# Other transfer and load times in a schedule table, and new seeds, in a two-layer MoE kernel behind attention

## The chip, the core and the metric

The kernel runs on one core of one Trainium2 chip. The metric is the device time of one execution in microseconds (us). Of the kernel before there are three timed executions and one more that was profiled.

The engines are named as the profile names them: PE is TensorE (PEld its weight loads), ACT is ScalarE, DVE is VectorE, POOL is GpSimd, SP is SyncE. Each engine works through its own list of instructions in the order in which the program put them there, and waits at an instruction whose inputs are not ready.

## The reference

Causal attention on 2 x 12 heads of 448 positions and 64 columns, then two feed-forward layers on the 896 tokens, each 768 to 2048 to 768:

```python
scores = scale * np.matmul(q, k.transpose(0, 1, 3, 2))
scores = np.where(mask, -1000000000.0, scores)
...
attn = attn / (np.sum(attn, axis=-1, keepdims=True) + 1e-09)
x = np.matmul(attn, v)                       # heads side by side: 896 x 768

h = x @ w_in                                 # layer 0
x = (h * np.clip(h + 3.0, 0.0, 6.0) / 6.0) @ w_out
h = x @ w_in2                                # layer 1
y = (np.maximum(h, 0.0) + alpha * np.minimum(h, 0.0)) @ w_out2
```

The four weight matrices are float64, everything else is float32.

## The kernel before

**Attention.** `attend` handles a head pair of both batches, six times: scores (line 496), the row maximum on DVE (447), exponentials on ACT (452), normalising on POOL or DVE (467 to 476), transposes on PE (521), copies of these from PSUM to SBUF on ACT or DVE (547 and 554), and the product with v (565).

**The two layers** use a seven-product scheme for 2 x 2 blocks instead of eight. Every product multiplies a sum of weight blocks by a sum of activation blocks, and every float32 operand is split in a high and a low part, so that `three` (584) issues three matmuls of 448 columns for each 128 x 128 block. Layer 0 and layer 1 have the same shape: first `w_in`, eight pairs of row blocks, 63 matmuls each, then `w_out`, seven products of 72 matmuls in the order 1, 2, 7, 6, 4, 5, 3.

**Preparing weights.** `convert` loads a block of float64 words (SP, 259) into one of three `raw` buffers and makes float32 of it in two ACT instructions (262 and 265) and one on DVE (268). In `w_in` the sums of blocks are `s12` (599 and 601) and two sums in place, made by `add_on`: `w1 += s12` and `w2 += w1`. Then come casts to the high part on ACT (617) and the subtraction that gives the low part on DVE (618). The products' tiles are named after these: `a1`, `s12`, `s4`, `s3`, `a2`; the pair's results stand in the PSUM banks `a`, `b` and `c` and are copied out by ACT (319 and 321, to a tile `g`) before the bank takes the next product; the results are then added up (650) and passed through the activation function (660 to 668). In `w_out` the right-hand sides of products 7, 6 and 4 are sums in place of `g` tiles (again `add_on`), split into `x70h`, `x60h`, `x40h` and so on (283 on ACT, 290 on DVE), and its weights are `w7h`, `w6h` and so on.

**A sum in place** (`add_on`, 301) has two forms: a DMA that adds to its destination, issued by POOL (307), or an addition on DVE (309).

**The order** is worked out by a planner in the kernel (`Plan.solve`, 113). It keeps a time for each engine and takes, step by step, the instruction that can start first, the earlier due time first. Each operation carries a cost in us. A transfer is counted as landing `WAIT[cols]` plus 0.0025 us a column after its issue, a load after the two numbers in its `.lands(...)`, and due times are counted back through these. For a sum in place the planner chooses the engine:

```python
if POOL in o.dma and done_by(*o.on[0]) + o.on[-1][1] <= o.due - EARLY:
    ok = e == POOL
else:
    ok = e == min(o.on, key=lambda c: done_by(*c))[0]
```

So it is a transfer if that would be done 3 us (`EARLY`) and one addition before it is due, and otherwise goes to whichever of the two is done first. The due times of the attention's operations are shaken by a random number generator started from each of `SEEDS` in turn.

Of the kernel before, what the change touches and what calls it, by code (L numbers as in the profile page):

```python
# [24 lines left out]
W3 = HK * P  # L25
# [7 lines left out]
PE, DVE, ACT, POOL, SP = "PE", "DVE", "ACT", "POOL", "SP"  # L33


def f32(t):
    return t.bitcast(F32)
# [23 lines left out]

ISSUE, WAIT = 0.9, {384: 2.2, 448: 4.6, 768: 4.2}

TURN = {("r", "r"): 0.05, ("r", "t"): 0.17, ("r", "c"): 0.2, ("r", "q"): 0.15, ("r", "m"): 0.15, ("t", "r"): 0.12,
        ("t", "c"): 0.12, ("t", "q"): 0.1, ("m", "c"): 0.2, ("m", "r"): 0.1, ("m", "q"): 0.1}
# [14 lines left out]
class Plan:  # L82
# [4 lines left out]
    def op(self, on, emit, reads=(), writes=(), due=FAR, chain=None, also=(), port=False, mode=None):  # L87

        o = Op(on if isinstance(on, list) else [on], emit, due)
        o.port, o.mode = port, mode  # L90
        for key in reads:
            w, r = self.state.setdefault(key, ([], []))
            o.before.update(w)
            r.append(o)
        for key in writes:
            w, r = self.state.setdefault(key, ([], []))
            o.before.update(w)
            o.before.update(r)
            self.state[key] = ([o], [])
        o.before.discard(o)  # L100
        for key in (*reads, *writes, *also):
            b = key[0] if isinstance(key, tuple) else key
            if b not in o.bufs:
                o.bufs.append(b)
                b.left += 1
        if chain:
            if chain in self.last:
                o.before.add(self.last[chain])
            self.last[chain] = o
        self.ops.append(o)  # L110
        return o
# [127 lines left out]
class Kernel:  # L239
# [9 lines left out]
    def convert(self, src, sign=1.0, halves=False):  # L249

        nc, op = self.nc, self.plan.op
        raw = Buf("raw", "raw", 2 * DM, U32)
        w = Buf("w", "wf", DM, U32)
        keys = [(w, 0), (w, W3)] if halves else [w]

        def words(k):
            return raw.tile.rearrange("p (n two) -> p n two", two=2)[:, :, k]

        op((SP, 0.45), lambda e: nc.sync.dma_start(out=raw.tile, in_=src), writes=[(raw, "l"), (raw, "h")]).lands(2.3, 1.9)


        op((ACT, 0.80), lambda e: nc.scalar.activation(  # L262
            f32(w.tile), f32(words(1)), AF.Prelu, scale=sign * 2.0 ** -112, alpha=-2.0 ** 32), reads=[(raw, "h")], writes=keys)

        op((ACT, LOWEST), lambda e: nc.scalar.activation(  # L265
            words(0), raw.tile.bitcast(U16).rearrange("p (n four) -> p n four", four=4)[:, :, 1],
            AF.Copy, bias=-0.49999, scale=1.0 / 8192.0), writes=[(raw, "l")])
        op((DVE, 0.87), lambda e: nc.vector.scalar_tensor_tensor(  # L268
            out=w.tile, in0=w.tile, scalar=3, in1=words(0), op0=ALU.logical_shift_left, op1=ALU.bitwise_or),
           reads=[(raw, "l")], writes=keys, port=True)  # L270
        return w
# [26 lines left out]
        op(low_on, low, reads=[*keys, hi], writes=[lo], port=not ps)  # L298
        return hi, lo

    def add_on(self, out, cols, dst, src, reads, writes, send=False):

        nc = self.nc

        def emit(e):
            if e == POOL:
                nc.gpsimd.dma_start(out=dst(), in_=src(), accum_op=ALU.add)  # L307
            else:
                nc.vector.tensor_add(dst(), dst(), src())

        on = [(POOL, ISSUE), (DVE, 0.065 + 0.00105 * cols)]
        self.plan.op(on[:1] if send else on, emit, reads=reads, writes=writes, port=True).lands(WAIT[cols], 0.0025 * cols, on=POOL)

    def copy(self, out, src, key, cols, sign=1.0):
        nc = self.nc
# [276 lines left out]
    def w_in(self, layer, m, src, due):  # L592
        nc, op = self.nc, self.plan.op
        w1 = self.convert(src[m], -1.0, True)
        w2 = self.convert(src[m + PAIRS], 1.0, True)
        s12 = Buf("w", "s12", DM, F32)
        left, right = slice(0, W3), slice(W3, DM)

        op((DVE, 0.47), lambda _: nc.vector.tensor_add(s12.tile[:, right], f32(w2.tile[:, left]), f32(w2.tile[:, right])),  # L599
           reads=[(w2, 0), (w2, W3)], writes=[(s12, W3)], port=True)  # L600
        op((DVE, 0.47), lambda _: nc.vector.tensor_add(s12.tile[:, left], s12.tile[:, right], f32(w1.tile[:, left])),  # L601
           reads=[(s12, W3), (w1, 0)], writes=[(s12, 0)], port=True)

        def both(name, cols, src, keys):

            if cols == DM:
                hi, lo = Buf("w", name + "h", DM, F32R), Buf("w", name + "l", DM, F32R)
                parts = (hi, 0), (lo, 0)
            else:
                t = Buf("w", name, DM, F32R)  # L610
                parts = ((t, 0), 0), ((t, W3), W3)

            def out(i):
                key, first = parts[i]
                return (key[0] if isinstance(key, tuple) else key).tile[:, first:first + cols]

            op((ACT, 0.07 + 0.00087 * cols), lambda _: nc.scalar.copy(out(0), src()), reads=keys, writes=[parts[0][0]])  # L617
            op((DVE, 0.065 + 0.00105 * cols), lambda _: nc.vector.tensor_sub(out(1), src(), f32(out(0))),  # L618
               reads=[*keys, parts[0][0]], writes=[parts[1][0]], port=True)
            return parts  # L620
# [2 lines left out]
        p56 = both("s12", DM, lambda: s12.tile, [(s12, 0), (s12, W3)])  # L623
        p4 = both("a2", W3, lambda: f32(w2.tile[:, right]), [(w2, W3)])

        self.add_on(w1, W3, lambda: f32(w1.tile[:, right]), lambda: s12.tile[:, left], [(s12, 0)], [(w1, W3)], SEND > 1)
        self.add_on(w2, W3, lambda: f32(w2.tile[:, left]), lambda: f32(w1.tile[:, left]), [(w1, 0)], [(w2, 0)], SEND > 0)
        p7 = both("s4", W3, lambda: f32(w1.tile[:, right]), [(w1, W3)])
        p3 = both("s3", W3, lambda: f32(w2.tile[:, left]), [(w2, 0)])

# [193 lines left out]
WARM = 3  # L824
SPLIT = (0, 1)
SEND = 0
LOWEST = 0.85
SCALERS = 2
SEEDS = (21, 46993, 49846, 39502, 10980, 46964, 66667)
ATT = {"kq": 2 * S, "v": 8 * D, "e": 3 * P, "el": 4 * P, "small": 21, "a": 16 * P}  # L830


def solve(k):
    return k.plan.solve(SLOTS, ("u", "w", "raw"), ("u", OVER, set(ATT)), k.vary, SEEDS)

# [105 lines left out]
```

## Time and profile before

| | |
|---|---|
| three timed executions | 526.29, 525.88, 526.03 us (median 526.03) |
| the profiled execution | 521.06 us, its span from first to last instruction 519.0 us |
| busy share of the span | PE 96%, PEld 83%, DVE 82%, ACT 75%, POOL 25% |
| matmuls | 2598, of which 2016 in the two layers (line 584) |
| moved by DMA | 82.69 MB |

The span is one core's. Matmuls overlap in the pipeline, so the busy share of PE doesn't tell how near it is to its peak; idle time that the profile shows on PE is lost, though. The clock of PE (PEclk in the views) is 1.00 at the full 2.4 GHz and 0.50 at 1.2 GHz. Attention fills the first 84 us, `w_in` of layer 0 runs on PE from there to 193 us, `w_out` from 193 to 304, layer 1's `w_in` to 411 and its `w_out` to 516 us.

### The profile page before, as it was taken

Reading aid. Unit: us, or ns where it says so; the run is one execution under the profiler, and the core shown is the slowest. Engines: PE = TensorE matmul, PEld = TensorE weight load, DVE = VectorE, ACT = ScalarE, POOL = GpSimd, SP = SyncE. Lnnn points to the kernel's source line nnn. Section 1 sums busy time; section 2 is a strip of 40 time slices with the busy share of each in tenths; the row PEclk is TensorE's granted clock in tenths of the full one; section 3 lists DMA queues with packets and bytes.
Section 4 is the critical chain, followed back from the end, with each engine's and each line's share of the span. In section 5 each row is a group of like instructions: output and inputs, shape, how many; then the busy total and the mean of one; then the engine's idle time right before and its main releaser. Section 6 shows DMA issues by size and latency. Waiting matters only on the chain.

```text
span 519.0 us, 7641 instructions
## 1 busy us (share of the span) xinstructions
PE 496.6 (96%) x2598; PEld 429.2 (83%) x2598; DVE 425.1 (82%) x808; ACT 390.5 (75%) x756; POOL 128.7 (25%) x196
## 2 busy tenths in 40 slices
PE   8899999999799999998998897999999999989997
PEld 4575667989689999997997786889999999979996
DVE  5799989999588799878999986887787999699710
ACT  6999999888588799866966676777788997597101
POOL 2775884112111003621001011221210146200000
PEclk9999999999889999999999899999999999999999
DMA  8655300678766549998005436676764699930111
GB/s 273 261 197 167 90 21 24 189 216 218 188 168 167 192 136 276 256 267 251 11 0 153 136 85 162 188 204 148 198 160 153 200 258 273 249 75 1 54 53 53
DMA packets 27638, 82.69 MB, mean 159 GB/s; under 512 B 3152, under 2 KB 15184, under 8 KB 27600
## 3 DMA queue, kind: packets, MB, share of 16 engines
q1 hardware_dynamic: 15216, 61.76, 34.3%
q0 software_dynamic: 12384, 20.45, 22.4%
q8 instruction: 20, 0.33, 0.3%
q14 instruction: 18, 0.15, 0.1%
HBM read 59.00 MB, written 2.75 MB: 119 GB/s over the span
## 4 chain that ended last, share of the span: by engine, by line
PE 44%; DVE 27%; DMA 17%; issue 5%; ACT 5%; POOL 2%; DVEq 0%; POOLq 0%; ACTq 0%; SPq 0%
PE a L584 12%; PE ya L584 12%; DMA g<-g 8%; PE c L584 7%; DMA wf<-s 6%; DVE wf L268 4%; PE b L584 3%; PE yc L584 3%; PE o L565 2%; PE t L521 2%; PE s L496 2%; DVE e L447 2%; DVE g L662 2%; DMA raw<-w2o 1%; DMA raw<-w1o 1%
## 5 line engine op out<-in xcount | busy, mean ns | idle before, releaser
L307 POOL DMA_DIRECT2D g<-g x48 | 41.6, 925 | 146.2 <-DVE g L668 50.3
L268 DVE SCALAR_TENSOR_TENSOR wf<-wf,raw 128x768 uint32<-128x768 uint32 x64 | 60.9, 952 | 15.1 <-ACT wf L262 14.9
L265 ACT ACTIVATE raw<-raw 128x768 uint32<-128x768 uint16 x64 | 58.5, 916 | 4.5 <-DMA raw<-w2i 1.9
L262 ACT ACTIVATE wf<-raw 128x768 f32<-128x768 f32 x64 | 57.5, 903 | 2.8 <-DVE w3l L287 1.4
L307 POOL DMA_DIRECT2D wf<-wf x25 | 21.8, 871 | 133.5 <-DVE s L599 39.4
L452 ACT ACTIVATE e<-e,small 128x128 f32<-128x128 f32 (+2 forms) x72 | 36.0, 505 | 5.1 <-DVE small L447 4.9
L476 POOL TENSOR_SCALAR e<-e,small 128x256 f32<-128x256 f32 (+2 forms) x67 | 31.4, 492 | 15.6 <-DVE small L469 11.0
L447 DVE CUSTOM_DVE_ANT_0 e<-s,mask 128x384 f32<-128x384 f32 (+2 forms) x72 | 27.0, 419 | 6.1 <-PE s L496 5.5
L618 DVE TENSOR_TENSOR s<-wf,s 128x384 fp32r<-128x384 f32 x32 | 17.8, 570 | 10.2 <-ACT s L617 10.2
L319 ACT COPY o<-ya 128x448 f32<-128x448 f32 x3 | 1.6, 533 | 31.6 <-PE ya L584 31.6
L617 ACT CAST s<-wf 128x384 fp32r<-128x384 f32 x32 | 16.1, 507 | 12.0 <-DMA wf<-s 10.2
L565 PE MATMUL o<-a,v 128*64 128x448 f32 (+3 forms) x192 | 23.4, 386 | 0.0
L617 ACT CAST s12h<-s 128x768 fp32r<-128x768 f32 x16 | 13.3, 834 | 13.1 <-DVE s L601 13.1
L565 PEld LDWEIGHTS o<-a,v 128*64 128x64 f32 x192 | 12.7, 136 | 12.6 <-issue 5.2
L496 PE MATMUL s<-kq 64*128 64x384 f32 (+2 forms) x144 | 21.7, 405 | 1.3 <-DMA kq<-kq 0.8
L618 DVE TENSOR_TENSOR s12l<-s,s12h 128x768 fp32r<-128x768 f32 x16 | 15.8, 988 | 7.2 <-ACT s12h L617 6.7
L521 PE MATMUL t<-ident,e 128*128 128x128 f32 x144 | 19.0, 278 | 1.6 <-DVE small L447 1.1
L521 PEld LDWEIGHTS t<-ident,e 128*128 128x128 f32 x144 | 15.5, 141 | 5.5 <-POOL e L476 2.4
L496 PEld LDWEIGHTS s<-kq 64*128 64x128 f32 x144 | 11.6, 186 | 9.2 <-DVE small L447 3.2
L307 POOL DMA_DIRECT2D wf<-s x13 | 11.2, 864 | 25.3 <-DVE s L618 10.7
L668 DVE SCALAR_TENSOR_TENSOR g<-r,alpha,g 128x448 f32<-128x448 f32 x24 | 16.3, 679 | 0.9 <-ACT r L666 0.8
L319 ACT COPY g<-a 128x448 f32<-128x448 f32 x16 | 8.5, 531 | 10.3 <-PE a L584 10.1
(830 smaller groups left out, 1771.3 us busy)
## 6 DMA issues: line engine op xcount, KB each, us to landing
raw<-w1i SPq DMA_DIRECT2D x16, 768.0 KB, 5.4
raw<-w1o SPq DMA_DIRECT2D x16, 768.0 KB, 4.4
raw<-w2i SPq DMA_DIRECT2D x16, 768.0 KB, 4.5
raw<-w2o SPq DMA_DIRECT2D x16, 768.0 KB, 5.0
g<-g POOLq DMA_DIRECT2D x48, 224.0 KB, 9.1
kq<-kq SPq DMA_DIRECT2D x11, 448.0 KB, 5.3
wf<-wf POOLq DMA_DIRECT2D x10, 384.0 KB, 8.8
v<-v SPq DMA_DIRECT2D x12, 256.0 KB, 2.7
```

The source lines that it names most:

```text
L262: op((ACT, 0.80), lambda e: nc.scalar.activation(f32(w.tile), f32(words(1)), AF.Prelu, scale=sign * 2.0 ** -112, alpha=-2.0 ** 32), reads= ...
L265: op((ACT, LOWEST), lambda e: nc.scalar.activation(words(0), raw.tile.bitcast(U16).rearrange("p (n four) -> p n four", four=4)[:, :, 1], A ...
L268: op((DVE, 0.87), lambda e: nc.vector.scalar_tensor_tensor(out=w.tile, in0=w.tile, scalar=3, in1=words(0), op0=ALU.logical_shift_left, op1 ...
L307: nc.gpsimd.dma_start(out=dst(), in_=src(), accum_op=ALU.add)
L447: nc.vector.tensor_tensor_reduce(out=view(), in0=t.tile[:, off:off + cols], in1=self.mask[:, at:at + cols], scale=-SCALE, scalar=3.0e38, o ...
L452: nc.scalar.activation(view(), view(), AF.Exp, bias=small.tile[:, u:u + 1], scale=-1.0, accum_out=small.tile[:, 7 + u:8 + u])
L476: (nc.gpsimd if e == POOL else nc.vector).tensor_scalar(view(), view(), by, 1.0, ALU.mult, ALU.mult)
L496: nc.tensor.matmul(t.tile[:, off:off + (i + 1) * P], lhsT=kq.tile[rows, S + i * P:S + (i + 1) * P], rhs=kq.tile[rows, 0:(i + 1) * P], star ...
L521: nc.tensor.transpose(t.tile[:, at * P:(at + 1) * P], src.tile[:, off:off + P], self.ident)
L565: nc.tensor.matmul(o.tile[side * D:(side + 1) * D, 0:cols], lhsT=v.tile[:, (2 * kc + side) * D:(2 * kc + side + 1) * D], rhs=a.tile[:, at: ...
L584: nc.tensor.matmul(out, lhsT=t.tile[:, first + at:first + at + P], rhs=rhs.tile, start=start and key is hi and rhs is xh, stop=stop and ke ...
L618: op((DVE, 0.065 + 0.00105 * cols), lambda _: nc.vector.tensor_sub(out(1), src(), f32(out(0))), reads=[*keys, parts[0][0]], writes=[parts[ ...
```

## The change

The table `WAIT` counts transfers as landing later (for 384 columns 6.0 instead of 2.2 us, for 448 columns 6.5 instead of 4.6, for 768 columns 7.0 instead of 4.2), weight loads as landing after 3.2 + 2.4 instead of 2.3 + 1.9 us, and the second ACT instruction of `convert` at 0.81 instead of 0.85 us. `SEEDS` has four other numbers. `send` of `add_on` gets a third value (negative: always DVE); with `SEND = 0`, as before, the planner still chooses. What is computed stays the same.

```diff
-ISSUE, WAIT = 0.9, {384: 2.2, 448: 4.6, 768: 4.2}
+ISSUE, WAIT = 0.9, {384: 6.0, 448: 6.5, 768: 7.0}
...
-        op((SP, 0.45), lambda e: nc.sync.dma_start(out=raw.tile, in_=src), writes=[(raw, "l"), (raw, "h")]).lands(2.3, 1.9)
+        op((SP, 0.45), lambda e: nc.sync.dma_start(out=raw.tile, in_=src), writes=[(raw, "l"), (raw, "h")]).lands(3.2, 2.4)
...
-        op((ACT, LOWEST), lambda e: nc.scalar.activation(
+        op((ACT, 0.81), lambda e: nc.scalar.activation(
...
-    def add_on(self, out, cols, dst, src, reads, writes, send=False):
+    def add_on(self, out, cols, dst, src, reads, writes, send=0):
...
-        self.plan.op(on[:1] if send else on, emit, reads=reads, writes=writes, port=True).lands(WAIT[cols], 0.0025 * cols, on=POOL)
+        self.plan.op(on[:1] if send > 0 else on[1:] if send < 0 else on, emit, reads=reads, writes=writes, port=True).lands(WAIT[cols], 0.0025 * cols, on=POOL)
...
-SEEDS = (21, 46993, 49846, 39502, 10980, 46964, 66667)
+SEEDS = (21, 21752, 85156, 37451)
```

The order of the layers' matmuls on PE stays as it was; the attention's instructions are put in another order on every engine. Of the 104 sums in place 18 are on DVE before and 26 now, the others are transfers. All of the eight that moved are in `w_in` and have 384 columns: seven in layer 0 (pairs 1 and 3 to 6) and one in layer 1 (pair 1). In the attention three of the copies at line 547 and one at line 554 moved from DVE to ACT, and three normalisings from POOL to DVE; two copies at line 319 moved from ACT to DVE. Three places follow.

The first is POOL's list in layer 0, `w_in`, from the middle on. `s_1629`, `s_1694` and `s_1807` are the tiles `s12` of pairs 4, 5 and 6. Before:

```order
L307 DMA g_1552<-g_1532 128x448
L307 DMA wf<-wf 128x384
L307 DMA wf<-s_1629 128x384
L307 DMA wf<-wf 128x384
L307 DMA wf<-s_1694 128x384
L307 DMA g_1689<-g_1670 128x448
L307 DMA wf<-wf 128x384
L307 DMA wf<-s_1807 128x384
```

And now, the tiles having other numbers (`s_1924` is the `s12` of pair 7):

```order
L307 DMA g_1550<-g_1533 128x448
L307 DMA g_1681<-g_1666 128x448
L307 DMA wf<-wf 128x384
L307 DMA g_1813<-g_1793 128x448
L307 DMA wf<-wf 128x384
L307 DMA wf<-s_1924 128x384
```

The sums of pairs 4 and 5 have left POOL; they are additions at line 309 on DVE now.

The second is ACT's list in layer 1, `w_in`, at the end of pair 0 and the start of pair 1, with buffer numbers. `s4` is the cast that needs the sum of pair 2 (a transfer before and now); the last row copies the result of pair 1's first product out of PSUM. Before:

```order
L617 CAST s3_3484<-wf_3331 128x384
L617 CAST s4_3490<-wf_3290 128x384
L617 CAST a1h_3493<-wf_3438 128x768
L666 ACTIVATE r_3503<-g11_3404 128x448
L666 ACTIVATE g21_3511<-a_3370 128x448
L265 ACTIVATE raw_3457<-raw_3457 128x768
L321 ACTIVATE g11_3526<-a_3506 128x448
```

And now:

```order
L666 ACTIVATE r_3487<-g11_3390 128x448
L617 CAST a1h_3497<-wf_3433 128x768
L666 ACTIVATE g21_3505<-a_3364 128x448
L617 CAST s3_3507<-wf_3298 128x384
L617 CAST a2_3515<-wf_3298 128x384
L321 ACTIVATE g11_3522<-a_3492 128x448
L617 CAST s4_3527<-wf_3284 128x384
```

The copy and the activation of pair 0 stood behind the cast and stand ahead of it now.

The third is ACT's list in layer 0, `w_out`, ahead of product 6. `x44h`, `x45h` and `x46h` are split from sums in place for product 4, which comes after product 6. Before:

```order
L283 CAST x44h<-g_1902 128x448
L283 CAST x45h<-g_2031 128x448
L283 CAST x46h<-g_2150 128x448
L283 CAST w6h<-wf 128x768
L283 CAST x47h<-g_2297 128x448
L265 ACTIVATE raw<-raw 128x768
L262 ACTIVATE wf<-raw 128x768
L283 CAST w6h<-wf 128x768
```

And now:

```order
L283 CAST x44h<-g_1893 128x448
L262 ACTIVATE wf<-raw 128x768
L283 CAST w6h<-wf 128x768
L265 ACTIVATE raw<-raw 128x768
L283 CAST x45h<-g_2022 128x448
L283 CAST x46h<-g_2152 128x448
L283 CAST w6h<-wf 128x768
```

The first `w6h` stands ahead of `x45h` and `x46h` now; layer 1 has the same change of places. On DVE, finally, the additions at line 770 that end product 5 of layer 0 had a conversion (268), the subtraction for `a2` (618), a second conversion and an addition for `s12` (599) right ahead of them; now the last of these is the second conversion, and the 618 and the 599 come after.

## Rows read from the trace of the kernel before

**Rows 1.** Busy time by stretch: length; PE, PEld, DVE, ACT, POOL busy; clock; DMA.

```profile
20.00:120.00 100.00, 98.85 (x667) 73.07 (x666) 90.75 (x252) 92.97 (x242) 49.57 (x87) 1.00 0.43 131
...
120.00:180.00 60.00, 56.26 (x258) 50.61 (x257) 46.08 (x75) 46.48 (x76) 10.43 (x13) 0.94 0.67 183
...
240.00:284.00 44.00, 42.63 (x210) 38.84 (x208) 43.20 (x66) 34.31 (x57) 2.58 (x3) 1.00 0.28 78
```

**Rows 2.** PE in order of time, its six longest pauses, in brackets with releaser.

```profile
134.23 0.53 PE L584 MATMUL a<-t400h,a 128*128 128x448 f32 x1 [1.80 <-DVE g L650]
...
143.48 0.48 PE L584 MATMUL a<-t200h,s12h 128*128 128x448 f32 x1 [1.94 <-ACT g L321]
...
243.97 0.47 PE L584 MATMUL ya<-x62h,w6l 128*128 128x448 f32 x1 [1.34 <-DVE w6l L290]
...
287.63 0.44 PE L584 MATMUL ya<-x30h,w3h 128*128 128x448 f32 x1 [3.65 <-DVE y L770]
...
323.97 0.47 PE L584 MATMUL a<-t210h,s12h 128*128 128x448 f32 x1 [3.10 <-ACT g L321]
...
461.00 0.47 PE L584 MATMUL ya<-x62h,w6l 128*128 128x448 f32 x1 [1.27 <-DVE w6l L290]
```

**Rows 3.** PE's clock behind three pauses: stretch, length, PE busy, granted clock, DMA.

```profile
134.00:138.00 4.00, 3.77 (x11) 0.57 0.38 84
...
288.00:292.00 4.00, 4.00 (x14) 0.57 0.96 260
...
324.00:328.00 4.00, 4.00 (x19) 1.00 0.61 206
```

**Rows 4.** ACT in order of time, layer 0 and layer 1.

```profile
131.54 0.51 ACT L617 CAST s<-wf 128x384 fp32r<-128x384 f32 x1 [2.52 <-DMA wf<-s]
...
141.74 0.51 ACT L617 CAST s<-wf 128x384 fp32r<-128x384 f32 x1 [3.41 <-DMA wf<-s]
...
142.89 0.54 ACT L321 ACTIVATE g<-a 128x448 f32<-128x448 f32 x1
...
320.55 0.51 ACT L617 CAST s<-wf 128x384 fp32r<-128x384 f32 x1 [3.87 <-DMA wf<-s]
```

**Rows 5.** The chain that ended last: transfers, start and us to landing.

```profile
125.22 6.30 DMA wf<-s
...
224.02 12.33 DMA g<-g
...
312.26 8.21 DMA wf<-s
...
327.11 3.81 DMA wf<-s
```

**Rows 6.** Groups by line: count, busy us, mean ns, idle before and releasers.

```profile
L309 DVE TENSOR_TENSOR wf<-wf,s 128x384 f32<-128x384 f32 x3 | 1.7, 555 | 0.1
...
L547 ACT COPY a<-t 128x512 f32<-128x512 f32 x28 | 15.3, 585 | 1.0 <-PE t L521 0.9
...
L265 ACT ACTIVATE raw<-raw 128x768 uint32<-128x768 uint16 x64 | 58.5, 916 | 4.5 <-DMA raw<-w2i 1.9 <-DMA raw<-w2o 1.2 <-DMA raw<-w1o 0.6
```

**Rows 7.** ACT in order of time, layer 0 ahead of product 6.

```profile
236.38 0.57 ACT L283 CAST x46h<-g 128x448 fp32r<-128x448 f32 x1 [4.06 <-DMA g<-g]
...
236.85 0.83 ACT L283 CAST w6h<-wf 128x768 fp32r<-128x768 f32 x1
```

**Rows 8.** DVE in order of time, ahead of products 6 and 3.

```profile
237.71 0.96 DVE L290 TENSOR_TENSOR w6l<-wf,w6h 128x768 fp32r<-128x768 f32 x1 [2.21 <-ACT w6h L283]
...
284.94 0.55 DVE L618 TENSOR_TENSOR a<-wf,a 128x384 fp32r<-128x384 f32 x1
...
286.39 0.56 DVE L599 TENSOR_TENSOR s<-wf 128x384 f32<-128x384 f32 x1
```

**Rows 9.** The chain that ended last: nine matmuls of a product, in both layers.

```profile
150.84 1.86 PE b L584 x9
...
343.22 1.83 PE b L584 x9
```

More of the change, by code (lines that the diff above doesn't have):

```diff
@@ L624, in w_in @@
         p4 = both("a2", W3, lambda: f32(w2.tile[:, right]), [(w2, W3)])
-        self.add_on(w1, W3, lambda: f32(w1.tile[:, right]), lambda: s12.tile[:, left], [(s12, 0)], [(w1, W3)], SEND > 1)
-        self.add_on(w2, W3, lambda: f32(w2.tile[:, left]), lambda: f32(w1.tile[:, left]), [(w1, 0)], [(w2, 0)], SEND > 0)
+        self.add_on(w1, W3, lambda: f32(w1.tile[:, right]), lambda: s12.tile[:, left], [(s12, 0)], [(w1, W3)], SEND)
+        self.add_on(w2, W3, lambda: f32(w2.tile[:, left]), lambda: f32(w1.tile[:, left]), [(w1, 0)], [(w2, 0)], SEND)
         p7 = both("s4", W3, lambda: f32(w1.tile[:, right]), [(w1, W3)])
@@ L826 @@
 SEND = 0
-LOWEST = 0.85
 SCALERS = 2
-SEEDS = (21, 46993, 49846, 39502, 10980, 46964, 66667)
+SEEDS = (21, 21752, 85156, 37451)
 ATT = {"kq": 2 * S, "v": 8 * D, "e": 3 * P, "el": 4 * P, "small": 21, "a": 16 * P}
```

## The prediction

> **What bounds the kernel now.** I read the busy time by stretch first. PE is the bound nearly everywhere: from 20 to 120 us it is busy 98.9 of 100 us, from 240 to 284 us 42.6 of 44 [rows 1]. The same matmuls have to run after the change, so only what PE loses can be won: its pauses, and what its clock loses behind them. The next view is therefore PE in order of time. Six pauses of over 1.2 us stand in it, together 13.1 us: 1.80 and 1.94 in layer 0's first half, 1.34 and 3.65 in its second, 3.10 and 1.27 in layer 1 [rows 2]. Behind three of them the granted clock falls to the lower level, 1.2 GHz, for a while. The mean over 134 to 138 us is 0.57, so 4 x 0.43 = 1.7 us are lost; the same behind the 3.65 us pause; none behind the 3.10 us one [rows 3]. Over 120 to 180 us the mean clock is 0.94, which is 3.6 us of 60 [rows 1], hence two such falls, one behind each of the pauses there: 3.4 us.
>
> What ended the pauses? The releasers named are ACT and DVE, but look at what these two did before. ACT stood at a cast (617) until a transfer landed: 2.52 us up to 131.54, 3.41 us up to 141.74, 3.87 us up to 320.55 [rows 4]. The copy that PE waited for at 143.48 came on ACT at 142.89, behind that cast [rows 4]; ACT takes its list in order. At 134.23 it is one step longer: the activations behind the cast are late, then DVE's. The chain of waits shows the transfers themselves: 6.30 us from issue to landing for the first, 8.21 us for the third [rows 5]. The table counted 2.2 + 0.0025 x 384 = 3.16 us. So it is no lack of engine time: the planner put instructions that PE needs behind casts whose input it believed to be there.
>
> **The change, part by part.**
>
> *Sums that become additions.* The two transfers that stop ACT in layer 0 are the `s12` sums of pairs 4 and 5; both are additions on DVE now. An addition of this form takes 0.56 us [rows 6], eight are 4.4 us of DVE. Seven lie in layer 0. From 120 to 180 us DVE is idle 60 - 46.1 = 13.9 us [rows 1], which covers them; the one in pair 1 falls in the stretch before 120 us, where DVE is busy 90.8 of 100 us [rows 1]. Without cover its 0.56 us would fall on PE. Gain: both pauses, 3.74 us, and both falls of the clock, 3.4 us. Bounds: nothing gained, or all 7.1; I take all, since what stopped ACT is gone.
>
> *The order in layer 1.* The transfer that stops ACT at 320.55 is pair 2's, and it stays a transfer. But counted at 6.96 us it moves its cast back: the copy that PE waits for, and the two activations, now stand ahead of the cast. Even if the landing stays where it is, the copy doesn't wait for it. Gain 3.10 us; bounds 0 and 3.10; I take 3.1.
>
> *The order ahead of product 6.* In layer 0 ACT waits 4.06 us for the sum of `x46h`, and `w6h` follows only at 236.85 [rows 7], although product 4 needs the one much later than product 6 needs the other. That sum took 12.33 us to land [rows 5]; the table counted 4.6 + 1.12 and now 7.6, still too little, but enough to put the first `w6h` ahead of `x45h` and `x46h`, in both layers. DVE idled 2.21 us for that `w6h` [rows 8]. PE's pauses of 1.34 and 1.27 us are for the low parts that follow. I take 2.3 of the 2.6 us, since the second `w6h` still stands behind `x46h`; bounds 0 and 2.6.
>
> *Product 3 of layer 0.* The 3.65 us pause is PE waiting for DVE's additions at 770. DVE is busy 43.2 of 44 us before it [rows 1], so it is late by what it did earlier. Now it starts up to 2.21 us sooner at product 6, and two subtractions and additions no longer stand ahead, 0.55 + 0.56 [rows 8]; against that PE comes 1.34 us sooner. What is left: 3.65 + 1.34 - 2.21 - 1.11 = 1.7 us. Pauses of this length drew a fall of the clock in layer 0, so I leave the fall in. Gain 2.0 us; bounds 0, and 3.65 + 1.7 = 5.3 if pause and fall both go.
>
> *The attention.* Its order is drawn anew. Three copies of 585 ns move to ACT [rows 6] with one of half the columns, some 2.1 us, and ACT is busy 93.0 of 100 us in that stretch [rows 1]. Half of it should find a gap: a loss of 1.1 us, bounds 0 and 2.1.
>
> *Loads counted longer, the ACT cost, `send`.* Loads are asked for a little sooner. No PE pause ends on a load, and ACT lost only 4.5 us to them in 64 conversions [rows 6], off PE's path; cost nothing, and if the three buffers hold a load up, at most those 4.5 us come back. 0.81 for 0.85 moves a tie here and there. The third value of `send` isn't used.
>
> *Waits that remain.* The table now counts 6.96 us for 384 columns where one landing took 8.21 [rows 5]; I add that difference once, 1.25 us, as a new pause somewhere. Bounds 0 and 4, three more of that kind.
>
> *Spacing.* Nine matmuls take 1.86 us in one part and 1.83 in another [rows 9], without another sign; over layer 0's 95 us that is 1.6 us. Which of the two a stretch gets I can't tell; it goes into the range, either way.
>
> **A rule that speaks against it.** Transfers of the same size landed in 3.81 us and in 8.21 us [rows 5], the short one close to the old table. By the Trainium skill, "DMA: Bandwidth & Descriptors", section "Anatomy of one DMA", a DMA issued by GpSimd takes about 2.0 us and its bytes at 436 GB/s, an estimate of 2.45 us for 192 KB. By that page the old table was already too high and the change would give nothing, 526 us. The trace disagrees with 6.30 and 8.21 us where it matters, and the measurement decides.
>
> **The sum.** From the profiled execution's 521.06 us (span 519.0, 2.1 around it): -3.74 - 3.4 - 3.1 - 2.3 - 2.0 + 1.1 + 1.25 = -12.2, which is 508.9. The timed median is 526.03, 5.0 above the profiled one; I take that distance as fixed, so **513.8 us**.
>
> **The rivals.**
>
> *Given back on DVE (519 to 522).* Layer 0's first half becomes 7.1 us shorter while DVE has 3.9 us more to do in it, and at product 6 DVE had no lead left. If the lead that the pauses gave can't be made up, the 7.1 us return as a pause at products 6 and 3: 513.8 + 7.1 = 520.9. For it: 43.2 of 44 us there. Against it: 13.9 us idle before, and the better order ahead of product 6. Chance 0.22.
>
> *The change doesn't do what it says (525 to 527).* If transfers mostly land as fast as the 3.81 us one, and ACT would have been late anyway, the pauses stay and only attention's 1.1 us is added: about 527. The row at 312.26 speaks against it. The Trainium skill's figure of above would imply this case. Chance 0.04.
>
> *Slower: the attention ends later (528 and more).* ACT and DVE are busy 93 and 91 of 100 us there, so a worse order goes through to PE at full price. It decides from 12.2 + 1.1 us of lost time, that is if ACT's idle time rises from 7 us to 20 of those 100. Its work is the same within 2 us, so I see no reason for so much. Chance 0.07.
>
> *Better (505 to 508).* The pause at product 3 goes with its clock fall, 3.4 us more, and the spacing comes out well, 1.6, and no new wait: 513.8 - 3.4 - 1.6 - 1.25 = 507.5. Chance 0.09.
>
> **How the numbers follow.** The forecast, 508 to 519, has 0.58. The range of 8 in 10 takes in the better case and most of the first rival: 506.5 to 521.5. A measurement of this kernel can tell about 0.2%, 1.05 us. Faster by more: 0.58 + 0.22 + 0.09 = 0.89; within: 0.04; slower: 0.07.
>
> **What would show it.** In the profile after: no ACT wait at line 617 of over 2 us in layer 0 and no PE pause at 134 and 143; the clock at 1.00 from 120 to 180 us; ACT's copy ahead of the cast at the start of pair 1 in layer 1, with no pause; `w6h` at line 283 without a long wait just before it; at product 3 a pause under 2 us. Wrong I would be if PE's pauses come back between 225 and 290 us with DVE at full load, or if ACT's idle time from 20 to 120 us grows from the 7.0 us of before to over 12.

## The result

| | before | after |
|---|---|---|
| three timed executions, median | 526.03 us (525.88 to 526.29) | 504.66 us (503.38 to 505.45) |
| the profiled execution, its span | 521.06, 519.0 us | 504.66, 502.9 us |

The ratio is 0.959, with a 95% interval of 0.9558 to 0.9622. Forecast were 513.8 us and 506.5 to 521.5: the direction was right, the time is 9.1 us below the forecast and 1.8 us below the range. A later comparison, of six executions of the kernel after with eleven of before, gave 507.13 us (503.24 to 510.26) and 0.9631 (0.9582 to 0.968).

Busy time of the kernel after by stretch; columns as in [rows 1], the last two stretches lie behind pauses:

```profile
20.00:120.00 100.00, 98.41 (x661) 73.33 (x660) 88.80 (x251) 94.19 (x243) 47.43 (x84) 1.00 0.39 121
120.00:180.00 60.00, 60.00 (x298) 55.64 (x296) 56.34 (x92) 53.95 (x92) 6.88 (x8) 1.00 0.65 197
230.00:274.00 44.00, 43.54 (x215) 40.04 (x215) 42.22 (x63) 34.92 (x58) 2.02 (x3) 1.00 0.34 88
218.00:222.00 4.00, 4.00 (x21) 3.71 (x21) 3.96 (x6) 4.00 (x8) 3.34 (x4) 1.00 1.11 241
278.00:282.00 4.00, 4.00 (x21) 3.72 (x20) 4.00 (x9) 3.19 (x7) 0.00 (x0) 1.00 0.54 197
```

From 120 to 180 us PE is never idle now, and the granted clock is 1.00, where it was 0.94 [rows 1]. DVE rose there from 46.1 to 56.3 us of 60. No stretch of this execution shows a lower clock, not even the last two.

PE in order of time, the pauses that the layers still have, in brackets with their releaser:

```profile
217.76 0.47 PE L584 MATMUL yc<-x70h,w7h 128*128 128x448 f32 x1 [2.33 <-DVE y L770]
...
232.27 0.47 PE L584 MATMUL ya<-x60h,w6l 128*128 128x448 f32 x1 [0.46 <-DVE w6l L290]
...
277.66 0.47 PE L584 MATMUL ya<-x30h,w3h 128*128 128x448 f32 x1 [1.75 <-DVE y L770]
...
427.43 0.47 PE L584 MATMUL yc<-x70h,w7h 128*128 128x448 f32 x1 [1.19 <-DVE y L770]
```

Against [rows 2]: those at 134.23, 143.48 and 323.97 are gone, product 6's are 0.46 and none, product 3's is 1.75 instead of 3.65. New are 2.33 and 1.19 us at product 7. Two lists say why. ACT in order of time ahead of the first of these:

```profile
205.16 0.57 ACT L283 CAST x61h<-g 128x448 fp32r<-128x448 f32 x1 [0.42 <-DMA g<-g]
208.32 0.57 ACT L283 CAST x62h<-g 128x448 fp32r<-128x448 f32 x1 [2.59 <-DMA g<-g]
211.32 0.57 ACT L283 CAST x63h<-g 128x448 fp32r<-128x448 f32 x1 [2.44 <-DMA g<-g]
211.79 0.83 ACT L283 CAST w7h<-wf 128x768 fp32r<-128x768 f32 x1
```

And DVE in order of time, there:

```profile
212.65 0.96 DVE L290 TENSOR_TENSOR w7l<-wf,w7h 128x768 fp32r<-128x768 f32 x1 [4.48 <-ACT w7h L283]
...
217.09 1.15 DVE L770 TENSOR_TENSOR y<-y,yb 128x448 f32<-128x448 f32 x2
```

It is the picture of [rows 7] once more: `x62h` and `x63h`, wanted by product 6, wait for sums in place and hold up `w7h`, wanted by product 7. DVE stands 4.48 us for it, and the additions that free PE's banks come late.

Groups of the kernel after (count, busy, mean ns, idle before):

```profile
L265 ACT ACTIVATE raw<-raw 128x768 uint32<-128x768 uint16 x64 | 58.6, 916 | 3.4 <-DMA raw<-w2i 3.4
L617 ACT CAST s<-wf 128x384 fp32r<-128x384 f32 x32 | 16.0, 513 | 0.1
...
L309 DVE TENSOR_TENSOR wf<-wf,s 128x384 f32<-128x384 f32 x7 | 3.9, 557 | 0.2
```

The casts of this group at 617, which waited 2.5 to 3.9 us a time in [rows 4] and 12.0 us in all, now wait 0.1 us in all; seven additions of an `s12` stand on DVE where three stood [rows 6].

### The profile page after: what moved, and what is told of

It reads as the page before. It is cut to its first block, busy times and chain, and to the rows that moved or that the text cites. A ratio compares the mean times of both kernels' runs of the same rounds, so it can differ in the third digit from the quotient of the medians.

```text
span 502.9 us, 7634 instructions
## 1 busy us (share of the span) xinstructions
PE 489.1 (97%) x2598; PEld 427.0 (85%) x2598; DVE 425.9 (85%) x816; ACT 390.8 (78%) x758; POOL 120.8 (24%) x186
## 4 chain that ended last, share of the span: by engine, by line
PE 32%; DVE 13%; DMA 2%; issue 2%; ACT 2%; DVEq 0%
PE ya L584 11%; PE a L584 9%; PE yc L584 6%; PE c L584 4%; DVE wf L268 2%; DMA g<-g 2%; PE b L584 2%; DVE g L668 1%; DVE w3l L287 1%; DVE w5l L290 1%; DVE w4l L290 1%; DVE g L707 1%; DVE g L650 1%; DVE wf L707 1%; DVE s L618 0%
## 5 line engine op out<-in xcount | busy, mean ns | idle before, releaser
L307 POOL DMA_DIRECT2D wf<-wf x21 | 18.3, 872 | 123.6 <-DVE s L599 63.9
L447 DVE CUSTOM_DVE_ANT_0 e<-s,mask 128x256 f32<-128x256 f32 (+2 forms) x72 | 27.1, 418 | 9.4 <-PE s L496 8.6
L476 POOL TENSOR_SCALAR e<-e,small 128x384 f32<-128x384 f32 (+2 forms) x64 | 30.3, 492 | 9.8 <-DVE small L469 8.5
L565 PEld LDWEIGHTS o<-a,v 128*64 128x64 f32 x192 | 12.8, 136 | 13.1 <-ACT a L547 5.3
L521 PEld LDWEIGHTS t<-ident,e 128*128 128x128 f32 x144 | 15.8, 141 | 5.6 <-POOL e L476 4.2
L666 ACT ACTIVATE r<-g 128x448 f32<-128x448 f32 x24 | 13.9, 580 | 7.8 <-DVE g L650 7.8
L496 PEld LDWEIGHTS s<-kq 64*128 64x128 f32 x144 | 12.2, 186 | 7.9 <-issue 3.0
L660 ACT ACTIVATE r<-g 128x448 f32<-128x448 f32 x24 | 13.9, 579 | 5.3 <-DVE g L650 5.1
L547 ACT COPY a<-t 128x512 f32<-128x512 f32 x31 | 16.4, 588 | 0.6 <-PE t L521 0.4
```

Of the source, the lines that this page charges most:

```text
L447: nc.vector.tensor_tensor_reduce(out=view(), in0=t.tile[:, off:off + cols], in1=self.mask[:, at:at + cols], scale=-SCALE, scalar=3.0e38, o ...
L476: (nc.gpsimd if e == POOL else nc.vector).tensor_scalar(view(), view(), by, 1.0, ALU.mult, ALU.mult)
L496: nc.tensor.matmul(t.tile[:, off:off + (i + 1) * P], lhsT=kq.tile[rows, S + i * P:S + (i + 1) * P], rhs=kq.tile[rows, 0:(i + 1) * P], star ...
L521: nc.tensor.transpose(t.tile[:, at * P:(at + 1) * P], src.tile[:, off:off + P], self.ident)
L565: nc.tensor.matmul(o.tile[side * D:(side + 1) * D, 0:cols], lhsT=v.tile[:, (2 * kc + side) * D:(2 * kc + side + 1) * D], rhs=a.tile[:, at: ...
```

## The experiments

Where a run keeps an order and changes single places, this stands behind the planner (the numbers name operations; what they are is said each time), and an operation whose inputs now come later follows them:

```diff
 def solve(k):
-    return k.plan.solve(...)
+    order = k.plan.solve(...)
+    for i in ON_DVE:
+        ops[i].eng = DVE
+    for i, j, after in MOVED:
+        order.remove(ops[i])
+        order.insert(order.index(ops[j]) + after, ops[i])
```

Each median is given with the lowest and highest execution, each ratio against executions of the kernel before beside it.

**The kernel before again, twice** (no edit).

> The kernel before, unchanged, with a new profile. If the 5 us between its profiled execution (521.06) and its timed ones (526.03) is a fixed distance, as the prediction took it, the new profile comes out near 521 again, with the same six PE pauses and three clock falls, while the timed executions stay at 526. If instead executions of this kernel differ in their pauses and clock falls, the timed executions or the new profile lie elsewhere between 519 and 527, and a profile that is slower than 521 shows where: another pause, or a clock fall behind one that had none (1.7 us each, so three would make 5).

> The kernel before once more, for another profile. So far its executions lie between 521.1 and 530.4 us, and the two profiled ones, at 521.06 and 523.47, differ by the length of the pauses (18.9 and 21.6 us in all) with the same 5.1 us lost to the clock. Theory: the 5 us between the first profile and the median are longer pauses and more clock falls, so a profile at 525 or more has 2 us more of one or the other for each 2 us; a profile near 521 has the pauses and the three falls of the first. Rival: something that the profile doesn't show, the same pauses and falls at 525 or more.

Measured: 526.04 us (521.26 to 530.41, ten), with a profile at 523.47; 528.38 us for the other, which was profiled. The latter's busy time by stretch, in and behind three pauses:

```profile
134.00:142.00 8.00, 5.94 (x17) 5.30 (x18) 6.91 (x12) 5.96 (x10) 1.72 (x2) 0.57 0.48 111
288.00:296.00 8.00, 6.71 (x20) 6.09 (x21) 7.53 (x15) 4.72 (x8) 0.86 (x1) 0.57 0.66 210
325.00:333.00 8.00, 6.34 (x18) 5.66 (x19) 5.95 (x8) 5.42 (x9) 1.72 (x2) 0.57 0.56 147
```

Its PE in order of time:

```profile
136.06 0.74 PE L584 MATMUL a<-t400h,a 128*128 128x448 f32 x1 [3.81 <-DVE g L650]
145.84 0.47 PE L584 MATMUL a<-t200h,s12h 128*128 128x448 f32 x1 [1.58 <-ACT g L321]
...
289.30 0.71 PE L584 MATMUL ya<-x30h,w3h 128*128 128x448 f32 x1 [4.74 <-DVE y L770]
...
326.66 0.74 PE L584 MATMUL a<-t210h,s12h 128*128 128x448 f32 x1 [3.04 <-ACT g L321]
```

Its ACT in order of time, and then one transfer of its chain of waits (start, us to landing):

```profile
133.37 0.51 ACT L617 CAST s<-wf 128x384 fp32r<-128x384 f32 x1 [5.26 <-DMA wf<-s]
```

```profile
125.02 8.32 DMA wf<-s
```

The same sum that landed in 6.30 us [rows 5] took 8.32 here; ACT waited 5.26 instead of 2.52 us, PE 3.81 instead of 1.80. And each of three falls of the clock cost 8 x 0.43 = 3.4 us, twice as much as in the first profile. One of them is at the pause at 326.66, which had drawn none before [rows 3]; the pause at 145.84 drew none this time. Together that is 10.2 us instead of 5.1. The six longest pauses make 16.0 us with 1.45 and 1.35 at product 6, against 13.1; all pauses together make 21.4 against 18.9 (table below). So 2.5 + 5.1 = 7.6 us of lost time stand for 528.38 - 521.06 = 7.3 us. The distance isn't fixed: it is the same waits, longer, and longer falls of the clock.

**Two sums on DVE, `s12` of pairs 4 and 5 in layer 0**, in the order of before:

```diff
+ON_DVE = (823, 880)
```

> The kernel before in its own order, with one thing changed: the two s12 sums of pairs 4 and 5 in layer 0 are additions on DVE, at the same place, and no transfers. Theory of the late landings: ACT's two waits of 2.5 and 3.4 us at the cast of line 617 go, PE's pauses of 1.80 and 1.94 us at 134 and 143 us go, and the two clock falls behind them (1.7 us each): 7.1 us less, about 514 against the profile of before and 519 against its timed median. Rival, given back on DVE: the pauses go, but product 6 and 3 of layer 0 wait longer for DVE (3.65 us becomes up to 10), and the time stays within 2 us of before. Second rival, ACT would have been late anyway: pauses stay.

Measured: 518.26 us (516.67 to 523.05), ratio 0.985 (0.9789 to 0.991), 8.0 us less. Its profile is of the slowest of the four executions (523.05), with five falls of the clock. ACT's waits at 617 in that stretch and both pauses are gone, but for 0.84 us at another matmul, and product 3 is not paid more. PE in order of time:

```profile
142.73 0.47 PE L584 MATMUL c<-b2200h,s 128*128 128x448 f32 x1 [0.84 <-ACT g L319]
...
284.32 0.71 PE L584 MATMUL ya<-x30h,w3h 128*128 128x448 f32 x1 [4.03 <-DVE y L770]
```

The 4.03 us are within what before shows by itself (3.65 and 4.74). The rival "given back on DVE" falls.

**The first `w6h` ahead of `x45h` and `x46h` on ACT**, both layers:

```diff
+MOVED = ((1259, 1367, 0), (2232, 2340, 0))
```

> The kernel before in its own order, with one cast moved in each layer: the first w6h stands ahead of x45h and x46h on ACT. Theory: the sum that w6h needs had landed 2.9 us before x46h's did, so PE's pauses at product 6 (1.34 us in layer 0; 0.26, 0.33 and 1.27 in layer 1) shrink to under 0.5 each and DVE, free earlier, shortens the 3.65 us at product 3 by up to 2.2: 2.3 to 4.5 us less. Rival: PE then waits for the second w6h or for x45l and x46l at product 4, and nothing is gained (within 0.5 us).

Measured: 525.33 us (520.33 to 528.84), ratio 0.9962 (0.9927 to 0.9996): about 1 us by the medians, at most 3.8 by the interval. That is nearer to the rival than to the theory's 2.3 to 4.5. The pause is where it was, since it waits for the second `w6l`. ACT casts the second `w6h` at 240.56 us, behind `x46h` and `x47h` as ever, which wait 3.33 and 1.81 us for their sums:

```profile
243.57 0.47 PE L584 MATMUL ya<-x62h,w6l 128*128 128x448 f32 x1 [1.43 <-DVE w6l L290]
...
460.29 0.47 PE L584 MATMUL ya<-x62h,w6l 128*128 128x448 f32 x1 [1.46 <-DVE w6l L290]
```

The kernel after has also moved the second one. ACT in order of time, the second `w6h` of before:

```profile
240.97 0.82 ACT L283 CAST w6h<-wf 128x768 fp32r<-128x768 f32 x1
```

And of the kernel after, with the `x47h` that it now stands ahead of:

```profile
231.72 0.82 ACT L283 CAST w6h<-wf 128x768 fp32r<-128x768 f32 x1
...
236.93 0.56 ACT L283 CAST x47h<-g 128x448 fp32r<-128x448 f32 x1
```

PE begins product 6 at 238.09 us in before and at 231.24 in the kernel after, so the cast comes 2.9 us behind that in one and 0.5 us in the other.

Nor did the moved cast help product 3: DVE's wait of 2.21 us [rows 8] is gone, but DVE now waits 0.70, 0.88 and 0.44 us there, and the pause at product 3 is 4.06 us.

**Both together, and pair 2's sum of layer 1 on DVE:**

```diff
+ON_DVE = (823, 880, 1685)
+MOVED = ((1259, 1367, 0), (2232, 2340, 0))
```

> The kernel before in its own order with the edits of the two runs above together, and pair 2's s12 sum of layer 1 on DVE as well: five small changes of an order of 2300 matmuls, no new seeds, no other table. If the late landings are the whole of the gain, this one comes to within 3 us of the kernel after: 7.1 + 2.3 + 2.0 + 3.1 = 14.5 less, so 506.5 against the profile of before; it also shows whether attention's new order and the loads' new numbers are worth anything. Rival: half of the gain or more comes from the new seeds and the rest of the new order, and this one stays above 513.

Measured: 513.74 us (511.74 to 515.26), ratio 0.9746 (0.97 to 0.9793). Five places of an order of 2300 matmuls bring 12.6 us, and the pause at 324 us is gone; but 6.6 us to the kernel after are left against its 507.13 and 9.1 against its 504.66, so the late landings in `w_in` aren't all of it. In its profile (511.74) the pauses make 10.8 us, hardly more than the 10.2 of the kernel after. The larger part of the 7.1 us between these two profiles is three falls of the clock, at 17, 239 and 283 us (5.1 us in all), where the kernel after has none.

**The new `WAIT` alone, the new `SEEDS` alone, and the kernel after with the old `SEEDS`:**

```diff
-ISSUE, WAIT = 0.9, {384: 2.2, 448: 4.6, 768: 4.2}
+ISSUE, WAIT = 0.9, {384: 6.0, 448: 6.5, 768: 7.0}
```

> The kernel before with the new WAIT table alone (old seeds, old load times, 0.85). Five single moves gave 12.5 us of the 21.6 (526.3 to 513.7). Theory that the table is the change: the sums of pairs 4 and 5 and the order at product 6 come out as in the kernel after, and the time is at most 513, nearer to 505 if the table also puts right what the five moves left (2.6 us at product 3, 1.46 and 1.47 at product 6). Rival, the seeds matter as much: it stays at 510 to 516, with the 1.15 us pause at 16 us of attention in its profile and a clock fall behind it in some executions.

> The kernel before with the new SEEDS alone. The theory of the table: transfers counted at 3.2 us still stop ACT in the layers, so pauses of 2 to 4 us and clock falls remain and the time is 518 to 527. Rival, the seeds are half of it: the pause at 16 us goes and the layers come out well by another draw, 515 or less.

> The kernel after with the old SEEDS: the new table, the new load times and 0.81 without the new attention order. Theory of the table: within 3 us of the kernel after (505 to 508), the rest being the 1.15 us pause at 16 us and the clock fall of 1.7 us that follows it in some executions. Rival: 510 to 516, the seeds carry what the five moves did not bring.

Measured: table alone 516.93 us (516.36 to 519.49), ratio 0.9859; seeds alone 516.27 (514.49 to 521.68), 0.9854; all but the seeds 509.15 (507.78 to 512.73), 0.9722. The table alone thus misses its 513, and what the loads and 0.81 add to it is 7.8 us, which no theory had. The other two lie between theory and rival. The seeds alone bring as much as the table alone: in their profile one of the two sums of `w_in` that stopped ACT in layer 0, pair 4's `s12`, is an addition on DVE too, at 127.43 us, with the old table, and the pauses at 134 and 143 us have shrunk to one of 0.47. Product 3 still pauses 3.68 us and layer 1 2.65, each with a fall of the clock. The parts don't simply add up, then: the table alone brings 8.1 us, the seeds alone 8.7 and the load numbers with 0.81 another 7.8, together 24.6, where the whole change brings 20.3 to 21.4.

The profile of the table alone shows where the load numbers were missing; ACT's waits by releaser (us in total, times, longest):

```profile
ACT raw L265 <- DMA raw<-w2i: 11.9, 6, 3.5
...
ACT raw L265 <- DMA raw<-w2o: 5.2, 3, 2.5
```

ACT in order of time at one of them:

```profile
369.05 0.88 ACT L265 ACTIVATE raw<-raw 128x768 uint32<-128x768 uint16 x1 [2.52 <-DMA raw<-w2o]
369.83 0.52 ACT L321 ACTIVATE g<-a 128x448 f32<-128x448 f32 x1
```

And PE's pauses in layer 1's `w_in`:

```profile
342.10 0.47 PE L584 MATMUL a<-t210h,s12h 128*128 128x448 f32 x1 [1.11 <-ACT g L321]
...
355.76 0.47 PE L584 MATMUL a<-t210h,s12h 128*128 128x448 f32 x1 [0.62 <-ACT g L321]
...
370.40 0.47 PE L584 MATMUL a<-t210h,s12h 128*128 128x448 f32 x1 [1.62 <-ACT g L321]
```

It is the copy behind the cast of [rows 4] again, now behind a conversion that waits for a load. With the sums out of the way ACT stands 17.1 us for loads of layer 1's weights, where it had lost 4.5 to all loads [rows 6].

**The kernel after with the old load numbers, and with the old `WAIT`:**

```diff
-... .lands(3.2, 2.4)
+... .lands(2.3, 1.9)
```

> The kernel after with the old numbers for the loads (2.3 + 1.9), all else new; attention's order is that of after. In the run with the new WAIT alone ACT waited 17 us at line 265 for loads, and three pauses of 1.11, 0.62 and 1.62 us in layer 1 ended on the copy right behind one. Theory, loads counted too short stop ACT as the sums did: those waits and pauses come back, 2 to 6 us more than the kernel after, 507 to 511. Rival, the prediction's own: loads cost nothing, within 1 us of the kernel after.

> The kernel after with the old WAIT table, all else new. Theory, the table is the larger part: ACT's waits at line 617 and PE's pauses behind them come back, with clock falls, 514 to 520. Rival: the new seeds and loads carry most, below 510.

Measured: 515.91 us (515.66 to 521.9), ratio 0.9831, without the load numbers; 513.93 (511.91 to 515.57), 0.9764, without the table. Both are needed. The first is 5 us slower than its theory had it. ACT waits at 265 for layer 1's `w_in` weights 11.9 us again, as in the table's run, and PE pauses behind it in layer 1:

```profile
316.27 0.47 PE L584 MATMUL a<-t210h,s12h 128*128 128x448 f32 x1 [0.78 <-ACT g L321]
...
356.47 0.47 PE L584 MATMUL a<-t210h,s12h 128*128 128x448 f32 x1 [0.90 <-ACT g L321]
...
370.56 0.47 PE L584 MATMUL a<-t210h,s12h 128*128 128x448 f32 x1 [1.05 <-ACT g L321]
```

At product 3 it pauses 4.49 us. Without the table ACT waits 5.7 us in all for sums at 617 (11.3 in before), 3.50 of them ahead of a pause of 2.27 us in layer 1. The planner makes a new order for each set of numbers, so these two runs and the three before them compare whole orders; the runs that keep an order and move single places show single causes.

**That order with six conversions moved** behind what they stopped, nothing else:

```diff
+MOVED = ((1671, 1622, 1), (1675, 1480, 1), (1785, 1641, 1), (1956, 1755, 1), (2013, 1812, 1), (2045, 1869, 1))
```

> The order of the run with the old load numbers (515.9), with six conversions of line 265 on ACT, each of which waited up to 3.0 us for a load, moved behind what they stopped: in layer 0's end behind a1h and behind the three casts b1110h to b1112h, in layer 1 behind the copies of lines 319 and 321. The loads themselves, DVE's and POOL's lists stay as they are. Theory, ACT's waits for loads are the cause: the pauses at 316, 356 and 370 us (2.7 in all) go, and the one at product 3 (4.49) shrinks by up to the 1.87 us of ACT's second wait there, with its clock fall of 3.4: 509 to 513. Rival, another draw of the order: within 1 us of 515.9, or the moved conversions are late for DVE and it is slower.

Measured: 511.82 us (510.73 to 512.35), ratio 0.971 (0.9657 to 0.9764): 4.1 us back by the medians, 6 by the ratios, in the theory's range. The three pauses in layer 1 are gone (one of 0.87 us has come up at another matmul), and product 3's has shrunk:

```profile
282.33 0.47 PE L584 MATMUL ya<-x30h,w3h 128*128 128x448 f32 x1 [2.92 <-DVE y L770]
```

So about 4 us of the difference to the kernel after are ACT's waits for loads; the rest (4.7 us against 507.13, 7.2 against 504.66) is not traced to one cause. Of the 7.7 us between this profile (512.35) and that of the kernel after, 2.7 are pauses, product 7's with 3.18 us the longest, and 5.1 the clock.

**The kernel after with places moved at products 7 and 3, then at product 6 too:** `w7h` ahead of `x61h`; at product 7 one 268, the 290 for `x64l` and one 707 behind the additions at 770; at product 3 of layer 0 one 268 and one 618 behind them; in the second run also `w6h` and `w6l` ahead of product 4's parts.

```diff
+MOVED = ((1199, 1265, 0), (2172, 2238, 0), (1401, 1172, 1), (1301, 1172, 1), (1276, 1169, 1), (2368, 2146, 1), (2274, 2146, 1),
+         (2249, 2144, 1), (1619, 1479, 1), (1574, 1479, 1))
...
+         (1259, 1350, 0), (1260, 1351, 0), (1278, 1367, 0), (1279, 1365, 0), (2232, 2323, 0), (2233, 2324, 0), (2251, 2340, 0), (2252, 2338, 0))
```

> The kernel after in its own order, with a few instructions moved: at product 7 in both layers w7h ahead of x61h on ACT, and on DVE one conversion, one subtraction for x64l and one line 707 behind the additions of line 770; at product 3 of layer 0 one conversion and one subtraction behind the additions. The pauses of the kernel after that end on line 770 are 2.33, 1.75 and 1.19 us. Theory, the casts x61h to x63h wait for sums that land 11 to 13 us after their issue and hold w7h up, as the w6h was held up before: the pauses shrink to under 0.5, 0.8 and 0.5, so 3.5 to 4.5 us less than the kernel after, about 500.5. Rival: what is moved back on DVE (conversions, x64l) is late at products 6 and 4 and the same time is lost there: 503 to 506.

> The run with moved instructions again, and at product 6 of both layers the first and second w6h ahead of the casts on ACT that wait for product 4's sums (x42h, x45h), and each w6l ahead of the low parts of product 4 on DVE. There the pauses of 1.90 and 1.53 us had come up when those at product 7 and 3 were gone. Theory, ACT's list is the whole cause: these two go as well, with none over 0.6 us in the layers, 3 us less, about 501. Rival, DVE and ACT have no lead left in w_out and the wait moves on to product 4 or 5: 504 to 506.

Measured: 505.75 us (504.27 to 508.02), ratio 0.964, for the first: nothing gained. The three pauses are gone and two have come up at product 6:

```profile
231.50 0.47 PE L584 MATMUL ya<-x60h,w6l 128*128 128x448 f32 x1 [1.90 <-DVE w6l L290]
...
440.78 0.47 PE L584 MATMUL ya<-x60h,w6l 128*128 128x448 f32 x1 [1.53 <-DVE w6l L290]
```

ACT stands there for the sums of `x42h` to `x44h`, as at product 7 for `x61h` to `x63h`. The second run took these away too: 503.78 us (502.89 to 504.05), ratio 0.9575, between its theory's 501 and its rival's 504 to 506; in its profile 1.84 us at product 3 are left, with a fall of the clock. The kernel after and this one, beside each other:

> The kernel after unchanged, for its spread and as the measure for the next run. Its first profile had 10.2 us of pauses and no clock fall, so its executions should lie within 3 us of each other, 503 to 506, against 9 us for the kernel before.

> The kernel after with the moves at products 7, 3 and 6, again, now beside the kernel after. Its first profile had 6.4 us of pauses and one clock fall of 1.7: 2.1 us less lost than the kernel after. If lost time costs one to one, its median is 1.5 to 3 us below that of the kernel after, and without the clock fall up to 3.8; rival, what is moved only spreads, and the two are within 0.5 us.

Measured: 507.13 us (503.24 to 510.26) for the kernel after, 503.32 (501.31 to 505.58) for the one with the moves, ratios 0.9631 (0.9582 to 0.968) and 0.9556 (0.9514 to 0.9597). It is 3.8 us faster by the medians, and the fastest version here, though the two intervals just overlap. The kernel after scatters by 7 us, not by the 3 expected: its new profile (506.04) has a clock fall of 1.7 us at product 7, behind a shorter pause than the 2.33 us that had drawn none:

```profile
218.11 0.74 PE L584 MATMUL yc<-x70h,w7h 128*128 128x448 f32 x1 [1.90 <-DVE y L770]
```

In the profile of the one with the moves only product 3 is left of the layers' pauses of over 0.5 us:

```profile
276.29 0.74 PE L584 MATMUL ya<-x30h,w3h 128*128 128x448 f32 x1 [3.26 <-DVE y L770]
```

**What the time consists of.** For each profile: PE's pauses of over 0.08 us added, half of the time at the lower clock (as far as it lies before PE's last matmul), and what is left of its time.

| profile | time | pauses | clock | rest |
|---|---|---|---|---|
| before | 521.06 | 18.9 | 5.1 | 497.1 |
| before again | 523.47 | 21.6 | 5.1 | 496.8 |
| before, third | 528.38 | 21.4 | 10.2 | 496.7 |
| `WAIT` alone | 516.36 | 18.8 | 0 | 497.5 |
| after, old seeds | 508.13 | 12.1 | 0 | 496.1 |
| after, old loads | 515.69 | 15.8 | 3.4 | 496.5 |
| after | 504.66 | 10.2 | 0 | 494.4 |
| after again | 506.04 | 7.3 | 1.7 | 497.0 |
| after, places moved (second time) | 504.64 | 8.1 | 3.4 | 493.1 |

The rest is 493.1 to 497.5 in all 17 profiles, while their times lie between 502.89 and 528.38 us: what is lost at pauses and to the clock accounts for the differences to within 4.4 us.

## Why the prediction was wrong

The step that failed is "The timed median is 526.03, 5.0 above the profiled one; I take that distance as fixed". The two further profiles of before show that such a distance is made of the very waits that the change removes or shortens: longer pauses than in the execution that I had read, and in the third profile longer falls of the clock. For the kernel after the distance is 0 in the first comparison (504.66 is both) and 1.1 us in the later one (506.04 profiled, 507.13 the median). Of 59 executions of before, between 521.06 and 530.41 us, the one profiled first was the fastest, so that the distance was as long as 5.0 us was bad luck as well. Left out, the forecast would have been the sum itself, 508.9, 4.2 us above 504.66 and 1.8 above 507.13: of the 9.1 us by which it missed, 5.0 are this step and 4.2 the terms below. The two medians of the kernel after are 0.5% apart, so the 0.2% that I said a measurement can tell was too little as well.

Point by point, from profile to profile (521.06 to 504.66, 16.4 us where 12.2 were forecast):

- *Sums that become additions*, 3.74 and 3.4: both came in full, and the run with these two sums alone shows the cause. DVE is busy 10.3 us more from 120 to 180 us and PE still has no pause there.
- *Layer 1*, 3.1: came in full; the single runs take the pause away by another means (the sum on DVE), so that the cast was the cause is shown, and that moving it back alone is enough is only seen in the kernel after.
- *Product 6*, 2.3: 0.46 us is left of the 1.34 in layer 0, none of the 1.27 in layer 1 and of two smaller ones (0.26 and 0.33) before it, so 2.7. The reason given, the first `w6h`, was wrong: moved alone it brought about 1 us, since PE waits for the second `w6l`, and the kernel after has the second `w6h` earlier too.
- *Product 3*, 2.0 with the clock fall kept: the pause shrank by 1.90 to 1.75 us where 1.7 were worked out, but the fall of 1.7 didn't come, so 3.6. That the pause came out right is in part luck. The run with the first `w6h` moved took DVE's wait of 2.21 us away, and the pause did not shrink; so that term of the working failed. That what stands right ahead of the additions counts, its other term, is borne out by the run that moves one 268 and one 618 behind them: no pause of over 0.25 us is left there.
- *Attention*, a loss of 1.1: none; ACT from 20 to 120 us is busy 94.2 instead of 93.0, and the first matmul of `t100h` starts at 81.80 instead of 81.90 us.
- *New waits*, 1.25: 2.33 + 1.19 = 3.5, at a place I hadn't looked at, and by the reason that I had given ("still too little") for the 448 columns.
- *Spacing*, left to the range: the items above make 3.7 + 3.4 + 3.1 + 2.7 + 3.6 - 3.5 + 0.1 = 13.1 us; 3.3 remain, of which 0.3 lie outside the span and 0.2 in smaller pauses. The others, some 2.8, are PE without a pause and at full clock. An estimated 1.7 of these are 436 matmuls between 148 and 239 us of before, which stand 206.7 ns apart and in the kernel after 202.7.
- *Loads, cost nothing*: this was wrong as an argument. The cover named, that ACT lost only 4.5 us to loads, held while ACT was late for other reasons. Without the load numbers the change brings 9 to 11 us less, of which the six conversions moved show 4 to be ACT's waits for loads. The sum was spared this error only because the change has both.

Of the rivals, "given back on DVE" fell with the two sums, "the change doesn't do what it says" with the result. By the Trainium skill, "DMA: Bandwidth & Descriptors", section "Anatomy of one DMA", the 192 KB sum would land in an estimated 2.45 us. The trace disagrees: the first one took 6.30 and 8.32 us in two executions of the same program, and the measurement decides. "Better, 505 to 508" came nearest, with a chance of 0.09, but only in part by its own terms: the fall at product 3 went and the spacing came out well, while the pause at product 3 stayed and the new wait was larger than in the sum. It too carried the 5.0 us.

What stays open: why the spacing comes out as it does, how much of the 21.4 us is the seeds' draw and how much the table's, and the part of the load numbers' worth that the six conversions don't explain.

## What to carry to other kernels

Before a distance between a profiled and a timed execution is carried over to another kernel, ask what it consists of: if the profile has waits for transfers, its executions can differ in these, and a change that removes the waits can remove the distance too (here 5.0 us before, 0 and 1.1 after). Where an engine takes its list in order, one landing counted too short stops everything behind it, and once that is put right, the next kind of landing that is counted too short (here loads, then the 448-column sums) takes its place; a cost hidden by a wait has to be priced again without that wait.

## What the hardware showed unexpectedly

- The same pause in the same program may or may not be followed by the lower granted clock: behind 3.10 us at 324 us none [rows 3], behind 3.04 us there in another execution 3.4 us lost. In the 17 profiles, past the first 20 us, the twelve longest pauses (3.18 to 5.44 us) all had a fall to 1.2 GHz in them or right behind them, 6 of the 16 between 2.19 and 3.10 us had one, and 7 of the 38 between 1.0 and 2.0.
- Transfers of one size and place land 2 us apart from one execution to the next (6.30 and 8.32 us), and a wait behind them passes this on.
- The distance between matmuls takes one of two values, and it changes mostly at a pause. PE in order of time in two executions of the kernel after, product 4 of layer 0 from its first matmul to the first of product 5, without a pause and with the clock at 1.00 in both. The first execution:

```profile
246.56 0.36 PE L584 MATMUL yc<-x40h,w4h 128*128 128x448 f32 x1
...
261.15 0.36 PE L584 MATMUL ya<-x50h,w5h 128*128 128x448 f32 x1
```

And the second one (506.04 us):

```profile
248.26 0.37 PE L584 MATMUL yc<-x40h,w4h 128*128 128x448 f32 x1
...
263.14 0.37 PE L584 MATMUL ya<-x50h,w5h 128*128 128x448 f32 x1
```

The same 72 matmuls take 14.59 us, 202.6 ns each, and 14.88 us, 206.7 ns each. Both executions had the closer distance from 96 us up to the pause at 218 us; after it the second keeps the wider one until its pause at 304.54 us, and has it again from its pause at 441.43 us to the end. These are 679 matmuls at some 4.0 ns more, an estimated 2.7 us, which is why its rest in the table is 497.0 and not 494.4. A pause isn't always at hand: in the profile of the table alone the distance changes at 121 and at 152 us, where PE has none. What decides it I can't tell.
